# A decode kernel's first weight load cut into 16 rows ahead of the opening barrier and 112 rows behind it

## The chip, the cores and the metric

The kernel runs on one core of a Trainium2 chip. The metric is the device time of one execution in microseconds (us); the median of several executions is quoted. A profile comes from one execution more. Its span runs from the first to the last instruction and is about 1.8 us shorter than the device time (406.7 of 408.51 us in the run profiled before the change).

Engines are named as in the profile: PE is TensorE's matmul, PEld its weight load, DVE is VectorE, ACT is ScalarE, POOL is GpSimd, SP is SyncE, which issues the loads here ("SPq" is its sequencer). The page counts 16 DMA engines for the core, which move the bytes; below, "DMA engine" always means one of those. They bring data from HBM (the large memory beside the cores) into SBUF (the core's own memory; the tiles of these loads have 128 partitions). A load reports its end to a semaphore, a counter that other engines wait on; that moment is its landing.

## The reference, cut to what matters

One token goes through a layer: layernorm, grouped-query attention over a cache of 65536 positions, then layernorm and a gated feed-forward block. Almost all of the time is reading weights and the cache.

```python
# x 1x1x1024; wq 1024x4096; k_cache, v_cache 1x4x65536x128; wo 4096x1024
# w_gate, w_up 1024x3584; w_down 3584x1024; all bfloat16
h  = x + attention(layernorm(x), k_cache, v_cache, wq, wo)
h2 = h + (gelu(layernorm(h) @ w_gate) * (layernorm(h) @ w_up)) @ w_down
```

That is 173 MB. The change touches only how the first 4 MB of `wq` come in.

## The kernel before: the parts that matter

All large data pass through one ring of five slots in SBUF, 32 KB per partition and slot. Every load goes through one helper, on SP's queue:

```python
    CW = 16384                       # elements per partition and slot
    NBUF = 5
    ...
    ring = chpool.tile([P, NBUF * CW], BF16, name="ring")      # P = 128
    ...
    def load(src, off=0):
        n, w = src.shape[1], src.shape[2]
        units = -(-(off + n * w) // CW)
        o = at[0] * CW + off
        assert o + n * w <= NBUF * CW
        at[0] = (at[0] + units) % NBUF
        tv = ring[:, o:o + n * w]
        nc.sync.dma_start(out=tv.rearrange("p (n w) -> p n w", w=w), in_=src)
        return tv.rearrange("p (n w) -> p n w", w=w)

    wq_v = A_wq.rearrange("(p c) n -> p c n", c=DC)            # DC = 8
    ...
    for c0 in range(0, DC, DC // 2):
        wq_t = load(wq_v[:, c0:c0 + DC // 2, :])
        wq_tiles.extend(wq_t[:, i, :] for i in range(DC // 2))
```

One such load of 128 rows (a row is what one partition gets) and 32 KB a row fills one slot; the first two loads are the two halves of `wq`. After the program is built, the very first load is moved from behind the opening barrier, at which all engines wait for each other, to the front of the program:

```python
    def first_load_leads(nc):
        ...
        first = ins.pop(at)          # SP's first instruction of the body
        assert isinstance(first, mybir.InstDMACopy) and not first.sync_info.on_wait
        ...
        head.insert(to, first)       # ahead of SP's part of the barrier
```

Of the kernel before, what the change touches and what calls it, by code (L numbers as in the profile page):

```python
# [17 lines left out]
def kernel(  # L18
# [13 lines left out]
    nc = tc.nc  # L32
    P = 128
# [6 lines left out]
    DC = D // P  # L40
# [116 lines left out]

    at = [0]

    def load(src, off=0):  # L160
        n, w = src.shape[1], src.shape[2]
        units = -(-(off + n * w) // CW)
        o = at[0] * CW + off
        assert o + n * w <= NBUF * CW
        at[0] = (at[0] + units) % NBUF
        tv = ring[:, o:o + n * w]
        nc.sync.dma_start(out=tv.rearrange("p (n w) -> p n w", w=w), in_=src)
        return tv.rearrange("p (n w) -> p n w", w=w)

    wq_v = A_wq.rearrange("(p c) n -> p c n", c=DC)  # L170
# [2 lines left out]
    assert DC * HD == 2 * CW and DC % 2 == 0  # L173
    wq_tiles = []
    for c0 in range(0, DC, DC // 2):
        wq_t = load(wq_v[:, c0:c0 + DC // 2, :])
        wq_tiles.extend(wq_t[:, i, :] for i in range(DC // 2))

    make_identity(nc, ident_bf[:])
# [12 lines left out]
    for bp in range(4):  # L192
        s0 = 64 * (bp // 2) + bp % 2
        nc.vector.tensor_copy(out=esel[:, bp, :, :],
                              in_=ident_bf[:, s0:s0 + 63:2].unsqueeze(1).to_broadcast([P, 4, 32]))
# [73 lines left out]
    def kv_load(what, g, li, n):  # L269
        t = load((k_v if what == "k" else v_v)[g][:, li * LN:(li + n) * LN, :])  # L270
        for u in range(n):
            state[(what, g, li + u)] = t[:, u * LN:(u + 1) * LN, :]
# [183 lines left out]
    for wc in range(Hq // WN):  # L456
        wv = load(wo_v[:, wc * WN:(wc + 1) * WN, :])
        for cc in range(WN):
            c = wc * WN + cc
            row_mm(at_ps, o2z[:, c, :], wv[:, cc, :], c, c < 4, c + 4 >= Hq)  # L460
# [80 lines left out]
    c0 = 0  # L541
# [39 lines left out]
```

## Time and profile before

| | before |
|---|---|
| device time, median of 5 runs | 408.56 us (408.39 to 408.72) |
| bytes read, mean rate over the span | 173.02 MB, 425 GB/s |
| time with 15 or more packets of the load queue in flight | 399 of 406.7 us |
| first packet starts, last packet of a load ends | 1.02 us, 402.8 us |
| a 32 KB packet in the steady stream | 1.21 us (1.23 us in the first rows) |

The third to fifth rows are counted from the trace's packet records. In these loads one packet is one row of 32 KB; the page counts 98.7% of 16 engines' span on the load queue. The page's lines are these: the span, the busiest compute engine, the load queue, the rate, and the issues of the `wq` loads (count, KB each, median us from issue to landing).

```profile
span 406.7 us, 2639 instructions
...
PE 295.0 (73%) x1481; PEld 63.6 (16%) x729; DVE 202.6 (50%) x185; ACT 44.7 (11%) x67; POOL 7.4 (2%) x17
...
q1 hardware_dynamic: 5192, 173.02, 98.7%
...
HBM read 173.02 MB, written 0.00 MB: 425 GB/s over the span
...
ring<-in_A_wq_dram SPq DMA_DIRECT2D x2, 4096.0 KB, 16.5
```

How to read it: the DMA engines are full from the first microsecond to the end. PE is 73% busy, but the loads never stop, so it isn't PE that sets the pace.

The timeline shows the start. Columns: start, duration, engine, line, operation, and in brackets how long the engine was idle and what ended that.

```profile
0.00 1.14 SPq L167 DMA_DIRECT2D ring<-in_A_wq_dram  x2
...
11.75 0.18 DVE L226 COPY xnz<-xn_bf 128x8 bf16<-128x8 bf16 x1
...
12.07 0.62 PE L145 MATMUL q_ps<-ring,xnz 128*32 128x512 bf16 x4 [1.72 <-DMA ring<-in_A_wq_dram]
...
21.74 0.62 PE L145 MATMUL q_ps<-ring,xnz 128*32 128x512 bf16 x4 [6.06 <-DMA ring<-in_A_wq_dram]
```

The first projection matmul waits for the first load (landed at 12.03 us), the 17th for the second (21.69 us). The trace has 16 landings for each of these loads; those of the first come from 11.61 to 12.03 us, and the matmul starts at 12.07 us, after the last of them. The chain of waits of the last microseconds begins with a load, too; columns: start, us, what.

```profile
372.48 30.02 DMA ring<-in_B_w_down_dram
402.49 0.04 issue
402.54 0.61 PE f_ps L145 x6
```

### The profile page before, as it was taken

What the parts mean: (1) busy time and instruction counts of PE and PEld (TensorE: products, weight loads), DVE (VectorE), ACT (ScalarE), POOL (GpSimd) and SP (SyncE); (2) the same over time, 40 slices, a digit from 0 to 9 for tenths busy, and PEclk for the clock granted to TensorE, in tenths of its full rate; (3) what the DMA queues carried; (4) which work ended last, traced back from release to release, by engine and by line L of the source; (5) the groups of instructions that cost most, each with busy time, mean ns of one, the idle gap of its engine ahead of it and who ended that gap; (6) DMA issues with size and microseconds to landing.
All of it is one profiled execution on the core that took longest, in us unless ns stands there. A gap on an engine that the chain in (4) does not pass through costs nothing.

```text
span 406.7 us, 2639 instructions
## 1 busy us (share of the span) xinstructions
PE 295.0 (73%) x1481; PEld 63.6 (16%) x729; DVE 202.6 (50%) x185; ACT 44.7 (11%) x67; POOL 7.4 (2%) x17
## 2 busy tenths in 40 slices
PE   0356766759976699598867978976597999626264
PEld 0021111111111012111111121111011111212032
DVE  1118999954979369146971960879424000221010
ACT  1010000032000040100001320000032000100000
POOL 2000000000000000000000000000100000100000
PEclk9999999888999899799898997999979799877665
DMA  9999999999999999999999999999999999999995
GB/s 368 458 413 461 414 416 458 420 429 440 416 464 419 409 500 414 413 422 425 487 414 419 432 442 419 414 480 413 471 419 419 446 393 445 430 442 426 426 419 220
DMA packets 5211, 173.18 MB, mean 426 GB/s; under 512 B 584, under 2 KB 592, under 8 KB 848
## 3 DMA queue, kind: packets, MB, share of 16 engines
q1 hardware_dynamic: 5192, 173.02, 98.7%
q8 instruction: 8, 0.13, 0.1%
q14 instruction: 3, 0.02, 0.0%
q10 hardware_dynamic: 8, 0.00, 0.0%
HBM read 173.02 MB, written 0.00 MB: 425 GB/s over the span
## 4 chain that ended last, share of the span: by engine, by line
DMA 62%; PE 27%; DVE 9%; ACT 1%; issue 0%; SPq 0%; ACTq 0%
DMA ring<-in_A_v_cache_dram 40%; PE acc_ps L147 12%; DMA ring<-in_A_k_cache_dram 7%; DMA ring<-in_B_w_down_dram 7%; DMA ring<-in_B_w_gate_dram 7%; DVE ring L281 7%; PE qk_ps L145 5%; PE qk_ps L147 5%; PE acc_ps L145 4%; DVE mx L302 2%; ACT sc L301 1%; PE wg_ps L145 0%; PE wg_ps L147 0%; PE f_ps L145 0%; DVE o_fin L549 0%
## 5 line engine op out<-in xcount | busy, mean ns | idle before, releaser
L281 DVE STREAM_TRANSPOSE ring<-ring 128x2048 uint32<-128x2048 uint32 x64 | 142.7, 2280 | 34.0 <-DMA ring<-in_A_k_cache_dram 34.0
L145 PE MATMUL qk_ps<-ring,wsel 128*128 128x512 bf16 x256 | 99.5, 389 | 35.5 <-DVE mx L302 23.6
L147 PE MATMUL acc_ps<-ring,pT 128*128 128x512 bf16 x384 | 115.0, 412 | 0.0
L147 PE MATMUL qk_ps<-ring,wsel 128*128 128x512 bf16 x256 | 99.5, 389 | 0.0
L145 PE MATMUL acc_ps<-ring,pT 128*128 128x512 bf16 x128 | 53.3, 416 | 17.8 <-DMA ring<-in_A_v_cache_dram 17.8
L145 PEld LDWEIGHTS <-wsel 128*128 128x128 bf16 x256 | 25.2, 98 | 133.6 <-issue 133.6
L301 ACT COPY sc<-qk_ps 128x1024 f32<-128x1024 f32 x16 | 16.2, 1011 | 177.2 <-PE qk_ps L147 177.2
L302 DVE TENSOR_REDUCE mx<-qk_ps 128x1 f32<-128x1024 f32 x16 | 19.5, 1222 | 25.4 <-ACT sc L301 25.4
L145 PEld LDWEIGHTS <-pT 128*128 128x128 bf16 x128 | 13.6, 106 | 117.5 <-issue 111.3
L357 DVE COPY acc_sb<-acc_ps 32x512 f32<-32x512 f32 x8 | 5.4, 671 | 34.5 <-PE acc_ps L147 34.4
L327 ACT ACTIVATE pe_r<-sc,nbias 128x1024 bf16<-128x1024 f32 x16 | 18.2, 1140 | 38.6 <-DVE nbias L322 37.9
L330 DVE STREAM_TRANSPOSE pT<-pe_r 128x1024 bf16<-128x1024 bf16 x16 | 19.0, 1227 | 6.2 <-ACT pe_r L327 6.2
L359 ACT COPY acc_sb<-acc_ps 32x512 f32<-32x512 f32 x8 | 4.6, 577 | 63.7 <-DVE acc_sb L357 63.7
L145 PE MATMUL q_ps<-ring,xnz 128*32 128x512 bf16 x32 | 5.2, 625 | 7.8 <-DMA ring<-in_A_wq_dram 7.8
L145 PE MATMUL f_ps<-ring,actz 128*32 128x256 bf16 x112 | 6.9, 415 | 5.4 <-DMA ring<-in_B_w_down_dram 5.4
L145 PE MATMUL o_ps<-sel,acc_sb 128*128 128x8 f32 x32 | 5.8, 309 | 6.5 <-DVE rl L371 5.7
L145 PE MATMUL wu_ps<-ring,hnz 128*32 128x512 bf16 x32 | 4.9, 527 | 7.5 <-DMA ring<-in_B_w_up_dram 7.5
L145 PE MATMUL wg_ps<-ring,hnz 128*32 128x512 bf16 x32 | 4.4, 492 | 8.1 <-DMA ring<-in_B_w_gate_dram 8.1
L145 PE MATMUL ln_tot<-ln_s,ones_f 128*128 128x1 f32 x8 | 1.9, 311 | 10.8 <-DVE ln_s L199 9.0
L315 DVE TENSOR_REDUCE gm<-mxT_ps 1x8 f32<-1x128 f32 x4 | 1.1, 279 | 15.0 <-PE mxT_ps L156 15.0
L237 DVE COPY q_ev<-q_ps 128x512 f32<-128x512 f32 x1 | 0.7, 691 | 13.4 <-PE q_ps L147 13.4
L145 PEld LDWEIGHTS <-hnz 128*32 128x32 bf16 x64 | 3.3, 116 | 21.8 <-issue 17.4
(102 smaller groups left out, 86.6 us busy)
## 6 DMA issues: line engine op xcount, KB each, us to landing
ring<-in_A_k_cache_dram SPq DMA_DIRECT2D x16, 4096.0 KB, 34.5
ring<-in_A_wq_dram SPq DMA_DIRECT2D x2, 4096.0 KB, 16.5
ring<-in_A_wo_dram SPq DMA_DIRECT2D x2, 4096.0 KB, 28.8
ring<-in_B_w_gate_dram SPq DMA_DIRECT2D x1, 7168.0 KB
ring<-in_B_w_up_dram SPq DMA_DIRECT2D x2, 3584.0 KB, 30.7
ring<-in_B_w_down_dram SPq DMA_DIRECT2D x1, 3584.0 KB, 37.4
ring<-in_B_w_down_dram SPq DMA_DIRECT2D x1, 1792.0 KB
ring<-in_B_w_down_dram SPq DMA_DIRECT2D x1, 1024.0 KB, 29.2
```

Of the source, the lines that this page charges most:

```text
L145: return pe(t.matmul(out, lhsT=lhsT, rhs=rhs, start=start, stop=stop, tile_position=tile_position, skip_group_check=skip_group_check))
L147: op = t.add_instruction(mybir.InstMatmult(name=nc.get_next_instruction_name(), engine=t.engine, start_tensor_calc=start, stop_tensor_calc ...
L237: nc.vector.tensor_copy(out=dst, in_=src)
L281: dv(nc.vector.transpose(out=kt[:, c * w:(c + 1) * w], in_=kt[:, c * w:(c + 1) * w]))
L301: ac(nc.scalar.copy(out=sc[:], in_=flat))
L302: dv(nc.vector.tensor_reduce(out=state[("mx", g)][:, li:li + 1], in_=flat, axis=AX.X, op=ALU.max))
L315: dv(nc.vector.tensor_reduce(out=gm[:], in_=mxT_ps[:].rearrange("o (x h) -> o h x", h=rep), axis=AX.X, op=ALU.max))
L327: ac(nc.scalar.activation(out=pe_r[:], in_=state.pop(("sc", g, li))[:], func=ACT.Exp, bias=nbias[:, 0:1], scale=scale, accum_out=lpart[:, ...
L330: dv(nc.vector.transpose(out=pT[:].rearrange("p m c -> p (m c)"), in_=pe_r[:]))
L357: dv(nc.vector.tensor_copy(out=acc_sb[sl, :], in_=acc[sl, c, :]))
L359: ac(nc.scalar.copy(out=acc_sb[sl, :], in_=acc[sl, c, :]))
```

## The change

The intent: the load ahead of the barrier becomes small. SP should then have less to issue before the barrier and the 16 DMA engines get 16 rows to start on; the other 112 rows are issued behind the barrier, while the first are on the way.

```diff
-    def load(src, off=0):
+    def load(src, off=0, cuts=(0, P)):
 ...
-        nc.sync.dma_start(out=tv.rearrange("p (n w) -> p n w", w=w), in_=src)
+        for p0, p1 in zip(cuts, cuts[1:]):
+            nc.sync.dma_start(out=tv[p0:p1].rearrange("p (n w) -> p n w", w=w), in_=src[p0:p1])
 ...
-        wq_t = load(wq_v[:, c0:c0 + DC // 2, :])
+        wq_t = load(wq_v[:, c0:c0 + DC // 2, :], cuts=(0, 16, P) if c0 == 0 else (0, P))
```

The order of instructions on PE, DVE, ACT and POOL is the same in both; SP has one load more, and the waits on the first load's data wait for two semaphores instead of one.

## The prediction

> **What bounds the kernel now.** The DMA engines. The page puts the one load queue at 98.7% of 16 engines' span, 173.0 MB at 425 GB/s. From the packet records of the trace I counted packets in flight: 16 or more during 398 of the 406.7 us, without a gap from 1.02 us (first packet) to 402.8 us (last). A row of 32 KB takes one DMA engine 1.232 us; 16 such rows at once are 425 GB/s, the kernel's whole rate. TensorE (73% busy) and VectorE (50%) wait for data inside this stream. So any microsecond by which every DMA engine starts earlier, or is held up, goes to the end nearly one to one; even one held-up engine counts, as each load waits for all 16.
>
> **What the change intends.** The first load is issued before the opening barrier: SyncE's issue takes 0.392 us, its drain ends at 0.574 us, the barrier opens at about 0.68-0.73 us and the second load is issued at 0.805 us. First packets of the 16 engines start between 1.02 and 1.82 us but all end near 3.05 us (2.79 to 3.21).[...]  The other 112 rows are issued at about 0.7 to 0.8 us. The extra issue costs 0.33 us on SyncE, hidden behind the queue. Intended gain: 0.3 to 0.7 us, all critical.
>
> **What I think it costs.** [...] The latest engine counts, though the last load's landings already differ by 1.6 us before, which may hide some. Afterwards no engine can catch up, since the queue never runs empty. Expected: +5 to +8 us in that case.
>
> **Prediction.** 414.2 us, with 408.6 to 417.2 us for 8 in 10. Faster by over 2%: 1%; within 2%: 77%; slower by over 2%: 22%.
>
> **What would show it.** Packet records: the first 16 packets take about 5 us each instead of 1.3 to 2.1[...], or end near 2.3 us (intent alone). Packets of the 112 rows spread between 1.2 and 3 us. First weight load lands at 15 to 19 us instead of 12.03, the second at 25 to 29 instead of 21.7; all later landings keep that shift; the 16 landings of each load spread over several us. Bytes moved unchanged, mean rate down by 1 to 2%.
>
> **What would make it wrong.** [...]

The sum behind the 414.2 us was +5 to +8 us, the last sentence of "What I think it costs". What is left of the sum in the record is the intended gain of 0.3 to 0.7 us, of which 0.7 had been subtracted; the author's reading of the start behind that gain, which no trace showed either, is cut, and so are the cases of "What would make it wrong". "Intent alone" is the case that only the gain occurs.

## More of the kernel before

The view by windows gives, for stretches in us from the span's start, the busy time of each engine, then the granted clock of PE (1.00 is full speed), the mean DMA share and the GB/s moved. A packet is booked whole at its start, so shares over 1 (1.06 in the first line) and odd rates in short windows mean nothing; stretches of many packets are good.

```profile
1.00:5.00 4.00, 0.00 (x0) 0.00 (x0) 0.21 (x3) 1.49 (x2) 2.46 (x5) 1.00 1.06 393
5.00:20.00 15.00, 4.77 (x36) 1.88 (x21) 3.12 (x18) 0.00 (x0) 0.82 (x2) 1.00 1.00 430
20.00:40.00 20.00, 12.28 (x65) 3.67 (x38) 9.69 (x7) 1.61 (x5) 0.00 (x0) 1.00 1.01 437
```

## The result, and the profile after

| | before | after |
|---|---|---|
| device time, median of 5 runs | 408.56 us | 417.61 us (417.13 to 417.69) |
| ratio of the fast runs | | 1.0221, 95% interval 1.0206 to 1.0236 |
| first load has landed in full | 12.03 us | 21.91 us |
| second load has landed | 21.69 us | 31.54 us |
| last load has landed | 403.13 us | 412.36 us |

Ratios, here and below, are the mean time of one kernel's fast runs over that of the other's of the same rounds, so not quite the ratio of the medians quoted. Slower by 9.05 us (the difference of the medians). That lies outside the predicted range, by 0.4 us, and over the 2% line on which 22% had been put.

The same lines of the page:

```profile
span 415.9 us, 2640 instructions
...
q1 hardware_dynamic: 5208, 173.02, 98.7%
...
HBM read 173.02 MB, written 0.00 MB: 416 GB/s over the span
...
ring<-in_A_wq_dram SPq DMA_DIRECT2D x1, 4096.0 KB, 30.4
ring<-in_A_wq_dram SPq DMA_DIRECT2D x1, 3584.0 KB, 21.1
...
ring<-in_A_wq_dram SPq DMA_DIRECT2D x1, 512.0 KB, 7.2
```

The bytes are the same and so is the busy share of 98.7%: the busy share hides the loss completely, because a DMA engine that gets on slowly counts as busy. The landing of the 512 KB, 7.2 us after the issue, is the first sign: at the rate of the page before they would need 1.2 us of transfer. By windows:

```profile
1.00:5.00 4.00, 0.00 (x0) 0.00 (x0) 0.21 (x3) 1.49 (x2) 2.46 (x5) 1.00 1.29 188
5.00:20.00 15.00, 1.17 (x4) 1.00 (x4) 3.11 (x18) 0.00 (x0) 0.82 (x2) 1.00 0.97 243
20.00:40.00 20.00, 8.68 (x76) 2.56 (x44) 1.08 (x3) 1.61 (x5) 0.00 (x0) 0.81 1.00 424
```

The rate is about halved up to 20 us, and normal from there on. (From 40 to 400 us it is 432 GB/s before and 433 after.) The timeline and the end of the chain:

```profile
0.00 1.60 SPq L168 DMA_DIRECT2D ring<-in_A_wq_dram  x3
...
17.45 0.18 DVE L227 COPY xnz<-xn_bf 128x8 bf16<-128x8 bf16 x1
...
22.04 0.62 PE L145 MATMUL q_ps<-ring,xnz 128*32 128x512 bf16 x4 [5.99 <-DMA ring<-in_A_wq_dram]
```

```profile
382.07 29.67 DMA ring<-in_B_w_down_dram
411.74 0.04 issue
411.79 1.04 PE f_ps L145 x11
```

PE starts at 22.04 instead of 12.07 us. (The input for it, `xnz`, is late as well, 17.45 instead of 11.75 us, because the load of `x` lands later: the first instruction on it starts at 12.89 instead of 7.19 us; it is not the last to come.) The later loads land 8.7 to 9.9 us later than before.

The packet records, in groups of 16 by start time, since about 16 are in flight at a time (15 or more during 399 us before the change). All packets are 32 KB.

```
                before: starts, mean us of a packet (min to max)     after
rows 1          1.02 to 1.82   1.78 (1.26 to 2.09)     1.02 to  1.90   3.73 (3.02 to 4.41)
rows 2          2.79 to 3.21   1.23 (1.22 to 1.25)     4.08 to  5.56   2.91 (2.63 to 3.71)
rows 3          4.01 to 4.44   1.21 (1.21 to 1.21)     7.49 to  8.19   2.26 (2.24 to 2.30)
rows 4          5.22 to 5.64   1.21 (1.21 to 1.21)     9.77 to 10.52   1.78 (1.54 to 2.21)
rows 5          6.43 to 6.85   1.21 (1.21 to 1.21)    11.66 to 12.55   1.86 (1.81 to 2.21)
rows 6          7.64 to 8.06   1.21 (1.21 to 1.21)    13.49 to 14.37   2.03 (1.79 to 2.34)
rows 7          8.85 to 9.27   1.21 (1.21 to 1.22)    15.28 to 16.60   2.22 (2.15 to 2.30)
rows 8         10.06 to 10.48  1.21 (1.21 to 1.21)    17.45 to 18.74   2.09 (2.00 to 2.24)
rows 9 (next)  11.28 to 11.70  1.21 (1.21 to 1.21)    19.57 to 20.87   1.74 (1.41 to 1.95)
rows 10        12.49 to 12.90  1.21 (1.21 to 1.21)    21.52 to 22.53   1.21 (1.21 to 1.22)
```

Two things are to be seen. The 16 rows of the small piece are slow, as predicted. And in rows 2 to 8, the 112 rows, *all* 16 packets of a group are slow, none is at 1.21 us. The prediction had expected a spread from 1.2 to 3 us there.

The intended gain isn't there. From the instruction and packet records:

```
                                          before     after
SP: the leading issue takes                0.392     0.400 us
SP reaches the barrier (end of its drain)  0.574     0.575 us
POOL opens the barrier                     0.678     0.679 us
SP issues the next load                    0.805     0.804 us
first packets of the 16 engines start   1.02 to 1.82   1.02 to 1.90 us
```

An issue takes as long for 16 rows as for 128, and the first packets come no sooner. Whether the bytes of a started packet flow a little sooner can't be read here, because the packets are slowed.

### The profile page after: what moved, and what is told of

It reads as the page before. It is cut to its first block, busy times and chain, and to the rows that moved or that the text cites. A ratio compares the mean times of both kernels' runs of the same rounds, so it can differ in the third digit from the quotient of the medians.

```text
span 415.9 us, 2640 instructions
## 1 busy us (share of the span) xinstructions
PE 296.5 (71%) x1481; PEld 63.0 (15%) x729; DVE 202.5 (49%) x185; ACT 44.7 (11%) x67; POOL 7.4 (2%) x17
## 3 DMA queue, kind: packets, MB, share of 16 engines
q1 hardware_dynamic: 5208, 173.02, 98.7%
## 4 chain that ended last, share of the span: by engine, by line
DMA 54%; PE 31%; DVE 11%; ACT 2%; issue 1%; SPq 0%; ACTq 0%
DMA ring<-in_A_v_cache_dram 30%; PE acc_ps L147 11%; DMA ring<-in_A_k_cache_dram 10%; DVE ring L282 8%; PE qk_ps L145 7%; DMA ring<-in_B_w_down_dram 7%; DMA ring<-in_B_w_gate_dram 7%; PE qk_ps L147 7%; PE acc_ps L145 4%; DVE mx L303 2%; ACT sc L302 2%; PE wg_ps L145 0%; PE wg_ps L147 0%; DVE pT L331 0%; ACT pe_r L328 0%
## 5 line engine op out<-in xcount | busy, mean ns | idle before, releaser
L145 PE MATMUL qk_ps<-ring,wsel 128*128 128x512 bf16 x256 | 101.1, 395 | 35.5 <-DVE mx L303 23.6
L147 PE MATMUL qk_ps<-ring,wsel 128*128 128x512 bf16 x256 | 101.0, 395 | 0.0
```

Source lines behind the costliest of these rows:

```text
L145: return pe(t.matmul(out, lhsT=lhsT, rhs=rhs, start=start, stop=stop, tile_position=tile_position, skip_group_check=skip_group_check))
L147: op = t.add_instruction(mybir.InstMatmult(name=nc.get_next_instruction_name(), engine=t.engine, start_tensor_calc=start, stop_tensor_calc ...
```

## The experiments

**Theory (destination).** What counts is which SBUF partitions a load covers. In the expectations bare figures are what this theory expected: estimates, of which the runs show the parts 1.21 us and, from p64_half on, 2.57 us, but not why a given set of partitions should have the one or the other. **Rivals.** (1) The split itself: one more issue and semaphore, or a small load ahead of the barrier. (2) The source: which HBM rows are read together. (3) Any load of fewer than 128 rows is slow. Within the destination theory a second question arose from the rows 2 to 8: (4) are all 16 DMA engines slow together ("coupled" in the expectations), or only some of them ("independent")? The 10 to 13 us in p64_low and the engines counted in p16_onepair and p16_permuted_pair are estimates, too. The labels of the runs: "pair" in them stands for nothing measured.

18 runs were made, and all gave the right result. Where four runs were timed, the median is given; the time of the kernel before is that of the same job (408.37 to 408.57 us).

### 1. The same split along the columns

```diff
+        cuts = cuts or (0, n)
+        for n0, n1 in zip(cuts, cuts[1:]):
+            nc.sync.dma_start(out=tv.rearrange("p (n w) -> p n w", w=w)[:, n0:n1, :], in_=src[:, n0:n1, :])
 ...
+        wq_t = load(wq_v[:, c0:c0 + DC // 2, :], cuts=(0, 1, DC // 2) if c0 == 0 else None)
```

> The first load again goes as two, the small one ahead of the barrier, but cut along the columns: 128 rows of 8 KB, then 128 rows of 24 KB. Same count of loads, issues and semaphores as the changed kernel. [...]408.3 to 408.8 us, the second weight load lands at 21.7 us as before. Rival (it is the extra issue, the extra semaphore, or a small load ahead of the barrier that costs): 415 to 418 us, the second weight load lands near 31 us.

Measured: 408.24 us against 408.43 (ratio 0.9994, 0.9978 to 1.0011). The second load lands at 21.90 us, as in the kernel before (21.69). The rate by windows stays whole:

```profile
1.00:5.00 4.00, 0.00 (x0) 0.00 (x0) 0.21 (x3) 1.49 (x2) 2.46 (x5) 1.00 1.05 391
5.00:20.00 15.00, 4.78 (x36) 1.74 (x21) 3.12 (x18) 0.00 (x0) 0.82 (x2) 1.00 1.02 442
```

Rival 1 falls: two pieces, a small one first and the rest behind the barrier, cost nothing here, where both cover all 128 partitions. They gain nothing measurable either (the 408.24 us are 0.06 us below the range that was written down).

### 2. The destination alone: the same 64 rows to other partitions

The probes add one load to the kernel *before*, behind the two weight loads, into a ring slot that is overwritten later. Nothing reads it. The stream is steady there, so its packets stand between packets of 1.21 us.

```diff
+    probe = ring[:, 4 * CW:5 * CW].rearrange("p (n w) -> p n w", w=HD)
+    nc.sync.dma_start(out=probe[0:64], in_=wq_v[0:64, 0:DC // 2, :])      # p64_half
+    # p64_mid: probe[32:96], wq_v[32:96]; p64_half_srcmid: probe[0:64], wq_v[32:96]
```

> Kernel before plus one extra 64-row load (32 KB a row, 2 MB) behind the two weight loads, into a ring slot that is overwritten later: partitions 0 to 63 from source rows 0 to 63. [...]packets of about 2.25 us instead of 1.23, total 408.56 + 4 x 2.25 = about 417.5 us. Source theory (HBM addresses of the rows set the pace): as p64_mid for other rows, no clear prediction, but it must follow the source rows. Theory that only bytes count: 408.56 + 4.93 = 413.5 us.

> The same extra 2 MB load, but partitions 32 to 95 from source rows 32 to 95. [...]packets of 1.23 us, total about 413.5 us. If any load of fewer than 128 rows is slow, whichever its partitions: packets of 2.2 us and about 417.5 us as in p64_half.[...]

> The same extra 2 MB load, destination partitions 0 to 63 as in p64_half, source rows 32 to 95 as in p64_mid. [...]the destination decides, packets of 2.25 us and about 417.5 us. Source theory: as p64_mid, whatever that is.

| run | partitions | source rows | probe's packets (32 KB) | time, minus before |
|---|---|---|---|---|
| p64_half | 0 to 63 | 0 to 63 | 2.57 us | 418.58, +10.15 us |
| p64_mid | 32 to 95 | 32 to 95 | 1.21 us | 413.18, +4.75 us |
| p64_half_srcmid | 0 to 63 | 32 to 95 | 2.57 us | 418.56, +10.13 us |

The 2.57 us are those of the second to fourth row; the first row overlaps the load before it (1.75 to 2.44 us). For p64_half 2.25 us and about 417.5 us had been expected; both were too low.

The windows of 21 to 31 us of the three, in this order; the last number is the rate in GB/s (in p64_mid the window begins and ends within other loads, and the 452 are an edge effect; 16 packets in 1.21 us are 433):

```profile
21.00:31.00 10.00, 4.97 (x44) 1.71 (x27) 1.08 (x3) 1.61 (x5) 0.00 (x0) 0.89 1.11 242
```

```profile
21.00:31.00 10.00, 5.14 (x44) 1.71 (x27) 1.08 (x3) 1.61 (x5) 0.00 (x0) 0.67 1.05 452
```

```profile
21.00:31.00 10.00, 5.07 (x44) 1.70 (x27) 1.08 (x3) 1.61 (x5) 0.00 (x0) 0.67 1.05 229
```

The same 2 MB cost 4.75 us or 10.15 us. The third run has the source of the second and the speed of the first: the destination decides, and rival 2 falls. The second is a load of half the rows at full speed: rival 3 falls. The 4.75 us are just the bytes (4 rows x 1.21 us = 4.84 us). To partitions 0 to 63 each packet takes 2.1 times as long (2.57 us instead of 1.21).

### 3. The two pieces of the change, each by itself

The same probe with `probe[0:16]` from `wq_v[0:16]`, and with `probe[16:128]` from `wq_v[16:128]`.

> Kernel before plus one extra load of 16 rows (512 KB) behind the two weight loads, partitions 0 to 15[...]. [...]packets of about 5.1 us, total 408.45 + 5.1 = about 413.5 us. Bytes only: packets of 1.21 us, total 409.7 us. This is the first half of the change, by itself.

> Extra load of 112 rows (3.5 MB), partitions 16 to 127: the second half of the change, by itself.[...] Bytes only: 408.45 + 7 x 1.21 = 416.9 us.[...] Engines coupled: packets near 2.1 to 2.57 us for all 16 engines, +15 to +18 us, 423.5 to 426.5 us (the changed kernel's own 112 rows took 15.2 us).

p16_near: 413.39 us, +4.82 us (ratio 1.0120, 1.0103 to 1.0137). Bytes alone would be 1.21 us, so these 16 rows lose 3.61 us. (512 KB in 4.82 us of added time are 109 GB/s; the 16 packets of 32 KB in 2.57 us of p64_half are 204 GB/s.) p112: 423.51 us, +14.94 us (1.0364, 1.0348 to 1.0379), where bytes alone would be 7 x 1.21 = 8.47 us: 6.47 us are lost. Its packets were 1.6 to 2.4 us, all 16 alike, as in the changed kernel. The window over the probe:

```profile
21.00:36.00 15.00, 4.87 (x44) 1.71 (x27) 1.08 (x3) 1.61 (x5) 0.00 (x0) 0.75 1.05 273
```

Both together: 4.82 + 14.94 = 19.76 us, and the undivided load takes 8 x 1.21 = 9.68 us, so the split should cost 10.1 us; at the landing of the first load it costs 9.88 us, in the total 9.05 us. The 112 rows are the larger part, and with +14.94 us they lie a little under what was written for coupled DMA engines (15 to 18 us).

### 4. Are all 16 DMA engines slowed, or only some? First looks

p64_low is the 64-row probe at partitions 16 to 79. p16_spread writes 16 rows to partitions 0, 7, 14 ... 105 (`probe[0:106:7]`).

> Extra load of 64 rows (2 MB), partitions 16 to 79[...]. Engines independent[...]; the latest engine then 10 to 13 us late, and the landings of the next loads spread by several us. Engines coupled[...]: all packets near 2.5 us, total about 418.5 us, landings close together.

> The same 16 source rows, written to partitions 0, 7, 14 ... 105[...]. A false dependency makes the next load wait for this one, so only the 16 packets count, not the total.[...] If the source rows or the row count decide: as p16_near, near 5 us.

p64_low: four runs at 418.60, 418.68, 421.93 and 440.26 us. The last is a slow run and the profile fell on it, and the third can't be explained, so only the two undisturbed times (+10.1 us) and the packets of the probe itself are used. The packets before it were the usual 1.21 us, those of the load after it 1.36 us, so the disturbance had begun by then. The second to fourth row of the probe took 2.53 to 2.59 us, for *all* 16 packets of each group. Had only some of the DMA engines been slowed, the others would have shown packets of 1.21 us. p16_spread was one look: its 16 packets took 1.72 to 2.08 us, none at 1.21 and none at 2.5 us. It doesn't settle the question, because the probe has only 16 packets, and they start up to 0.48 us apart, beside the last packets of the load before. Hence the next probe.

### 5. The same with short packets, in seven places

16 rows again, but each in 12 pieces of 7936 bytes, so that the middle packets meet only each other.

```diff
+    probe = ring[:, 2 * CW:5 * CW].rearrange("p (n w) -> p n w", w=HD)
+    nc.sync.dma_start(out=probe[0:106:7, :, 0:HD - 128],                   # p16_long
+                      in_=A_k_cache[0, 0].rearrange("(p n d) e -> p n (d e)", p=P, d=32)[0:16, 0:12, 0:HD - 128])
+    # p16_alone 32:96:4, p16_permuted 11:117:7, p16_onepair 36:100:4, p16_permuted_pair 15:121:7,
+    # p16_twopairs_up 40:104:4, p16_twopairs_down 24:88:4
```

The seven differ in the destination partitions only. (The next load has to wait for the probe here, so their totals are not used; each is a single look, of unknown state, but with packets of 1.21 us around it.)

> p16_spread again, but each of the 16 rows comes as 12 pieces of 7936 B, so that the middle packets are clear of the neighbouring loads.[...] Packet alone: 1.21 us x 7936 / 32768 = 0.29 us[...].[...] Engines coupled: all near 0.62 us. The total is disturbed by a false dependency and does not count.

> p16_long with the 16 rows written to partitions 32, 36, 40 ... 92 instead of 0, 7 ... 105[...]. Everything else, source rows too, as in p16_long. [...]middle packets back to 0.29 to 0.31 us for all 16. If 16-row loads or strided partitions are slow by themselves, or the source rows are: 0.61 us as in p16_long. The total is disturbed by a false dependency and does not count.

> As p16_alone, shifted by four partitions: 36, 40 ... 96.[...] Coupled engines: middle packets near 0.61 us for all 16. Independent engines: 14 at 0.30 us and 2 at 0.61 us.[...]

> p16_long with the 16 rows at partitions 11, 18 ... 116[...]. [...]middle packets 0.30 us for all 16, as in p16_alone. If an engine[...] is slower in itself[...]: 0.35 to 0.61 us. The total does not count (false dependency).

> The same shifted to partitions 15, 22 ... 120[...]. [...]as in p16_onepair: two engines at 0.67 us, 14 at 0.34 us.[...] The total does not count.

> Row pieces as in p16_long, partitions 40, 44 ... 100[...] (one step on from p16_onepair). [...]as in p16_long: middle packets 0.60 us for all.[...] The total does not count (false dependency).

> The same with partitions 24, 28 ... 84[...]. Same alternatives: 0.60 us for all 16[...].

The packets that start between 22.4 and 24.2 us, and the rate from the windows view of 22.5 to 24.5 us:

```
run                 partitions        packets: count x us                 GB/s
p16_alone           32, 36 ... 92     97 x 0.30                            425
p16_permuted        11, 18 ... 116    96 x 0.30                            421
p16_onepair         36, 40 ... 96     74 x 0.34, 5 x 0.67                  357
p16_permuted_pair   15, 22 ... 120    84 x 0.31, 6 x 0.62 or 0.63          385
p16_twopairs_up     40, 44 ... 100    45 x 0.63 to 0.66                    202
p16_twopairs_down   24, 28 ... 84     45 x 0.63 to 0.66                    202
p16_long            0, 7 ... 105      48 x 0.59 to 0.62                    214
```

The lines of p16_alone, p16_onepair and p16_twopairs_up in the windows view:

```profile
22.50:24.50 2.00, 2.00 (x24) 0.36 (x8) 0.00 (x0) 0.00 (x0) 0.00 (x0) 0.50 1.00 425
```

```profile
22.50:24.50 2.00, 2.00 (x24) 0.50 (x12) 0.00 (x0) 0.00 (x0) 0.00 (x0) 0.50 1.02 357
```

```profile
22.50:24.50 2.00, 2.00 (x28) 0.39 (x11) 0.00 (x0) 0.00 (x0) 0.00 (x0) 0.50 1.02 202
```

The destination decides here, too, and not by the spacing: of the four places with a spacing of 4 partitions one is fast (425 GB/s), one loses a little (357) and two run at half the rate (202); of the three with a spacing of 7 one is fast (421), one loses a little (385) and one runs at half (214). Where a little is lost, most packets stay near 0.30 us (0.34 and 0.31) and a few take about twice as long, 5 of 79 and 6 of 90. As an estimate from these durations, that many are what two of the 16 DMA engines make in the 1.8 us (2 x 1.8 / 0.67 = 5.4), and 14 others make 74 packets of 0.34 us. At half the rate *all* packets are slow, and 16 engines make 45 of 0.64 us. So the two rivals "coupled" and "independent" were too simple: p16_onepair and p16_permuted_pair look (nearly) independent, the last three coupled. p64_low agrees with the coupled ones for whole rows of 32 KB (2.53 to 2.59 us for all 16). Why a set of partitions belongs to one group or another is open; no run here shows the path between the DMA engines and SBUF.

For the 112 rows the mean packet of each group of 16 goes step by step like this (the changed kernel's rows 2 to 8; the seven rows of p112; rows 1 to 7 of cut_112_16 of the next section, whose 112 rows begin at partition 0):

```
step of the 112 rows                  1     2     3     4     5     6     7
partitions 16-127:
  changed kernel, mean us           2.91* 2.26  1.78  1.86  2.03  2.22  2.09
  p112, mean us                     1.85* 2.26  1.84  1.85  2.07  2.26  2.11
partitions 0-111:
  cut_112_16, mean us               1.95* 2.17  2.27  1.89  1.68  2.07  2.26
* mixed with the 16 rows or the load before it, or with the start of the stream
```

There is a dip to 1.78 to 1.86 us in steps 3 and 4, and it moves with the cut, to 1.89 and 1.68 us in steps 4 and 5. What sets it is not shown: the records name neither the engine nor the partition of a packet. No step is at 1.21 us.

### 6. Other cuts of the real load

Back in the changed kernel, only the cut positions differ: `(0, 64, P)`, `(0, 32, 96, P)` and `(0, 112, P)`.

> The changed kernel with its first load cut into 64 and 64 rows. [...]8 rows for each engine at 2.55 us = 20.4 us instead of 8 x 1.21 = 9.7 us, +10.7 us less some 0.6 us of start-up that is hidden: 418.6 us (418 to 419.3). Theory that it is the small uneven first piece (16 rows): back to about 408.5 us, or clearly less than the changed kernel's 417.6 us.

> The changed kernel with its first load cut into three: partitions 0 to 31, 32 to 95, 96 to 127. One piece more than the change. [...]2 rows at 2.55, 4 at 1.21, 2 at 2.55 = 15.0 us instead of 9.7 us: +5.4 us, less up to 0.6 us: 413.5 us (412.8 to 414.2). Theory that the count of pieces costs: slower than the changed kernel's 417.6 us.

> The changed kernel with the pieces in the other order: 112 rows ahead of the barrier, then 16 behind it. [...]+9 to +10 us: 417.4 to 418.6 us; the first packets take about 2 us, not 3 to 4. Theory that the harm comes from a short first load that leaves the queue short of work until the second is issued: back to about 408.5 us, since 112 rows keep the engines busy.

| run | pieces | time, minus before | expected by the destination theory |
|---|---|---|---|
| cut_64_64 | 0-63, 64-127 | 418.80, +10.28 us | 418 to 419.3 us |
| cut_32_64_32 | 0-31, 32-95, 96-127 | 413.64, +5.12 us | 412.8 to 414.2 us |
| cut_112_16 | 0-111, 112-127 | 417.74, +9.22 us | 417.4 to 418.6 us |

Their windows of 5 to 20 us, in this order:

```profile
5.00:20.00 15.00, 1.18 (x4) 1.01 (x4) 3.12 (x18) 0.00 (x0) 0.82 (x2) 1.00 1.02 210
```

```profile
5.00:20.00 15.00, 3.13 (x24) 1.51 (x16) 3.12 (x18) 0.00 (x0) 0.82 (x2) 1.00 0.98 315
```

```profile
5.00:20.00 15.00, 1.17 (x4) 1.00 (x4) 3.12 (x18) 0.00 (x0) 0.82 (x2) 1.00 1.05 227
```

All three fell in the ranges written beforehand. Three pieces cost half of what 64 and 64 rows cost (5.12 against 10.28 us): in the run with three the packets of the two outer pieces took about 2.6 us and those of the middle 1.21 us, in the rows that don't overlap another piece. With the large piece first the loss is the same (+9.22 us, the changed kernel +9.05), so neither the small size of the leading load nor a queue that runs short plays a part. None of the versions tried beats the kernel before; the column split of experiment 1 equals it.

## Why the prediction was wrong, point by point

- **"What bounds the kernel now": right.** The stream has no gap, and 9.88 us lost at the first landing were still 9.23 us at the last and 9.05 us in the time. In the mean over the 16 landings of a load the shift is 9.18 us at the first and 8.84 us at the last, so about half of the 0.65 us was hidden in the spread of the landings, as the prediction thought possible; the rest is open.
- **"So any microsecond ... goes to the end nearly one to one": right**, as the extra 4.84 us of bytes in p64_mid show, too (+4.75 us).
- **"Intended gain: 0.3 to 0.7 us": not there.** It rested on the reading of how the first packets start, which no trace showed. With 16 rows the issue took 0.400 instead of 0.392 us and the first packets started just as spread out, 1.02 to 1.90 us. That term had been subtracted from the cost. The pieces by themselves sum to 10.1 us and the first landing is 9.88 us late, so at most some 0.2 us can have been gained.
- **The loss of the 16 rows:** measured by itself, 3.61 us. The packets took 3.0 to 4.4 us rather than "about 5 us each"; part of the delay seems to show in the next packet (2.91 us on average).
- **The loss of the 112 rows: this is the step that failed, in size.** It came from an estimate in which the DMA engines didn't disturb each other. Measured by themselves the 112 rows lose 6.47 us. In them no packet of any engine was at the full speed of 1.21 us, and in three of the seven places with short packets all packets were at half speed (0.59 to 0.66 us instead of 0.30). The sum is then 3.6 + 6.5 - 0 = 10.1 us, of which 9.05 us arrive. Measured, the 16 landings of the first load are 8.8 to 9.9 us late, 9.2 us in the mean. How much of the miss is the disturbance can't be said; the gain that didn't come is up to 0.7 us of it.
- **Signs.** "Packets of the 112 rows spread between 1.2 and 3 us" and "the 16 landings of each load spread over several us" both failed for the same reason: the packets were 1.5 to 3.7 us, none at 1.21, and the first load's 16 landings came within 1.55 us (20.36 to 21.91). The landings of 21.91 and 31.54 us lie beyond the 15 to 19 and 25 to 29 us that were given. Right were the shift that stays, the unchanged bytes, and a mean rate down by about 2% (425 to 416 GB/s).
- **"What would make it wrong"**: missing was the case that occurred: all 16 packets of a group are slow in the 112 rows (1.5 to 3.7 us).

The lesson of the number: the upper bound of the range, 417.2 us, is +8.6 us, little more than the worst case (+8 us) of one estimate. Its weak point, that engines don't disturb each other, had no measurement behind it.

## What to carry to other kernels

Cut a load along its columns, not along its partitions: in this kernel the column split cost nothing (408.24 against 408.43 us), while pieces of part of the partitions ran at a quarter (16 rows at 0 to 15, 4.82 us instead of 1.21), half (64 rows at 0 to 63, 2.57 us a packet instead of 1.21) or 57% (112 rows at 16 to 127, 14.94 us instead of 8.47) of the full rate, and in this stream, which never pauses, 9.05 of the 9.88 us lost at the first landing went into the time. A load of a part of the partitions can be as fast as a whole one (here 32 to 95, 1.21 us a packet; 16 rows at 32, 36 ... 92, 425 GB/s), so measure a slice with a probe load before using it. A DMA busy share near 100% doesn't show such a loss (98.7% before and after); look at the duration of single packets and the rate by windows.
